# Blocks of x read by DMA already transposed, and another order of work in the last block, in a fused convolution and two-layer kernel

## The chip, the cores and the metric

The kernel runs on one core of one Trainium2 chip. The metric is device time in microseconds (us) of one execution, the median over several runs. Before the change it is 1195.06 us (three runs: 1194.38, 1195.06 and 1200.2). The profiled execution took 1194.39 us, of which the profile's span covers 1192.6 us.

## The reference

x has 2 x 4096 tokens of 192 features. Each of eight heads (24 features) has seven taps; softmax over the taps gives weights, and each token's feature is the weighted sum of itself and its six predecessors (zeros before the start of a sequence). Then come two feed-forward layers, 192 -> 2048 -> 192 each, with different functions between their products:

```python
x = attn_out.reshape(B * S, D)                  # causal 7-tap convolution of x
h = x @ w_in;  g = h * (1.0 / (1.0 + np.exp(-1.702 * h)));  x = g @ w_out
h = x @ w_in2; P = a[0] + a[1]*h + a[2]*h**2 + a[3]*h**3
Q = 1.0 + np.abs(b[0]) * np.abs(h) + np.abs(b[1]) * h**2
out = (P / (Q + 1e-06)) @ w_out2
```

## The kernel before, in words

The 8192 tokens are 16 blocks of 512 (T), numbered 0 to 15. Inside, features lie on partitions and tokens along the free dimension: a block is 128 features x 512 tokens ("main") and 64 features x 512 tokens ("side"), the latter folded to 128 x 256. So x must be transposed. `x_load` (L244) reads a block's rows as they are (one DMA of 256 KB, two of 64 KB) into `xn`; `x_halo` (L254) reads the six tokens ahead of the block, and of its second half, straight into the transposed tile `xt` by three DMAs with rearranged access patterns (L264 to L266); `x_transpose` (L269) turns the rest with six TensorE transposes (L275) and copies them from PSUM to `xt` with two ScalarE copies (L281, L282). `x_red` (L370) takes the block's largest magnitude from `xn` on VectorE (L373), `x_max` (L381) makes a scale of it, `x_conv_pool` (L325) does the convolution on GpSimd, and `x_high`, `x_low` (L403, L408) split the result into two halves of 16 bits.

Layer 1 is computed on split operands: `h_product` (L442) makes 128 x 1024 of a hidden product in one PSUM tile out of 24 matmuls (L423, L437); `gelu` and `g1_high`, `g1_low` follow; `o1_main` (L493) and `o1_side` (L504) make output product 1. Its result, rescaled by `scales` (L360) after a maximum over it (`x2_red_part` L556, `all_max` L83), is split by `high_part` and `low_part` (L347, L350) and enters layer 2: again `h_product`, then `unit` (L584: two ScalarE activations L591, L592, two VectorE operations L593, L594) and `denominator` (L597); `log` (L603) and `inverse` (L607), ScalarE functions of two different tables, and `quotient` (L611) give P / Q as a sigmoid of a logarithm; `o2_chunk` (L520) adds a sixteenth of output product 2 in float32 (L488). A hidden tile has eight steps (NS), a block sixteen chunks.

Work of several blocks is interleaved. All engines' orders are written by hand: each engine runs its instructions in the order in which the program issues them. The loop (L1003) has a turn for each block j from 0 to 14; with n1 = j+1, n2 = j+2 and conv = j+3, a turn holds:

- `x_load(conv)`, `x_halo(conv)` (L1007, L1008), all on the SP queue;
- the front part (`front_groups`, L763): hidden products of block n1 in layer 1 and of block j in layer 2, in groups of three PSUM tiles, with the chunks of block j-1 that are left. `extras` hangs further work on a step: `x_red(conv)` on step 2, `x_high(n2)` on 3, `x_low(n2)` on 4, `store(j-1)` on 6;
- the back part (`back_phase`, L803): `x_transpose(conv)` and `x_conv_pool(conv)`; output product 1 of n1 with the logarithms of block j beside it; scale and split of its result; the first products of the next front part; the quotients of block j.

On the SP queue the loads of a turn stand behind the `store` of the turn before, so they go out at the end of a front part, and what they bring is used in the next one. `xt` and `xn` have two buffers each. PSUM has eight banks: two for an output pair (`pair`, L302), six for three hidden tiles (`ps_h`).

The last turn calls `ending` (L654) instead of a back part. There output product 1 runs with all eight logarithms of block 14 beside it. Then the PSUM pool of three tiles is closed (L662) and replaced by two banks for block 14's output and two hidden tiles, so `product(i + 2)` waits for `readers(i)`:

```python
each(inverse, j, (0, 1))
quotient(j, 0)
o2_chunk(j, 0, 0)
```

After the split of x2, `product(i)` of block 15 alternates with one or two chunks of block 14 (L705 to L720); the quotients of block 15, its sixteen chunks and two half stores close the program.

Of the kernel before, what the change touches and what calls it, by code (L numbers as in the profile page):

```python
# [8 lines left out]
F32 = mybir.dt.float32  # L9
# [4 lines left out]
ALU = mybir.AluOpType  # L14
# [6 lines left out]
def kernel(  # L21
# [32 lines left out]
    tiny = ctx.enter_context(tc.tile_pool(name="tiny", bufs=3))  # L54
    ps_o = ctx.enter_context(tc.tile_pool(name="ps_o", bufs=1, space=bass.MemoryType.PSUM))

    ps_stack = ExitStack()
    ps_hs = [ps_stack.enter_context(tc.tile_pool(name="ps_h", bufs=3, space=bass.MemoryType.PSUM))]
    stack = ExitStack()
    stage = stack.enter_context(tc.tile_pool(name="stage", bufs=2))  # L60
    rings = []
# [192 lines left out]
    def x_halo(n, t=None):  # L254
# [11 lines left out]
        nc.sync.dma_start(out=t[D2:P, 0:HALO], in_=xf[first + TH - HALO:first + TH, P:D].rearrange("s d -> d s"))  # L266
        xt_t[n] = t

    def x_transpose(n):  # L269

        pt = ps_tile("pt")
        src, t = xn_t.pop(n), xt_t[n]

        def turn(dst, c):
            nc.tensor.transpose(out=dst, in_=src[:, c:c + P], identity=ident)  # L275

        for g in range(2):
            turn(pt[:, 1, g * P:(g + 1) * P], T + g * P)
        for g in range(NG):
            turn(pt[:, 0, g * P:(g + 1) * P], g * P)  # L280
        nc.scalar.activation(out=t[:, HALO:HALO + TH], in_=pt[:, 1, 0:TH], func=ACTF.Copy)  # L281
        nc.scalar.activation(out=t[:, 2 * HALO + TH:2 * HALO + W], in_=pt[:, 0], func=ACTF.Copy)  # L282
# [87 lines left out]
    def x_red(n):  # L370

        red = red_t[n] = tiny.tile([P, 2], F32, tag="red", name="red", bufs=4)
        nc.vector.tensor_reduce(  # L373
            out=red[:, 0:1], in_=xn_t[n], axis=AX.X, op=ALU.max, apply_absolute_value=True
        )
        if n * T % S:
            nc.vector.tensor_scalar(
                out=red[:, 1:2], in0=red[:, 0:1], scalar1=red_t[n - 1][:, 0:1], scalar2=None, op0=ALU.max
            )
# [140 lines left out]
    def o2_chunk(n, i, k, groups=range(NG)):  # L520
        pp = units_t[n][i][0]
        o_chunk(1, n, NS * k + i, ((pp, k, wo2[:, NS * k + i]),), groups)
# [27 lines left out]
    def x2_red(src):  # L550
        red = tiny.tile([P, 2], F32, tag="red2", name="red2")
        for j in range(2):
            x2_red_part(src, j, red)
        return red
# [48 lines left out]
    def log(n, i):  # L603
        qq = units_t[n][i][1]
        nc.scalar.activation(out=qq, in_=qq, func=ACTF.Ln, scale=ab[:, 15:16], bias=eps)  # L605
# [5 lines left out]
    def quotient(n, i):  # L611
        pp, qq = units_t[n][i]
        nc.vector.scalar_tensor_tensor(  # L613
            out=pp, in0=pp, scalar=ab[:, 0:1], in1=qq, op0=ALU.add, op1=ALU.mult
        )

    def each(f, n, steps):
        for i in steps:
            f(n, i)
# [33 lines left out]

    def ending(j, splits):  # L654

        n = j + 1
        for part in (o1_main, o1_side):
            for i in range(NS):
                o1_product(part, n, i, splits[i])
                if part is o1_main:  # L660
                    log(j, i)
        ps_stack.close()  # L662
        last = ctx.enter_context(tc.tile_pool(name="ps_last", bufs=1, space=bass.MemoryType.PSUM))
        po_t[1, j] = [last.tile([P, 512], F32, tag=f"l{k}", name="po") for k in range(2)]
        ps_hs.append(ctx.enter_context(tc.tile_pool(name="ps_two", bufs=2, space=bass.MemoryType.PSUM)))
        src = po_t.pop((0, n))
        each(inverse, j, (0, 1))
        quotient(j, 0)
        o2_chunk(j, 0, 0)
        pm = ps_tile("pm2")  # L670
        red = x2_red(src)
        all_max(red, pm)
        o2_chunk(j, 0, 1)
        sc = sc2_t[n] = tiny.tile([P, 24], F32, tag="sc2", name="sc2")
        scales(pm, sc, 2)
        xs = xs2_tiles(n)
        for p in (0, 1):
            high_part(src, sc[:, 1:2], xs, p)
        quotient(j, 1)
        for p in (0, 1):  # L680
            low_part(src, sc[:, 1:2], xs, p)
        each(inverse, j, (2, 3, 4, 5))
        x2_scales(sc, sc1_t.pop(n)[:, 6:7])
        each(quotient, j, (2, 3, 4, 5))
        phs = {}

        def product(i):
            phs[i] = h_product(1, n, i)

        def readers(i):  # L690
            pp = hl_tile().rearrange("p two t -> p (two t)").bitcast(F32)
            unit(n, phs.pop(i), pp)

        def own(m, i, groups=range(NG)):
            for k in range(2):
                o2_chunk(m, i, k, groups)

        first = NS // 2
        own(j, 1)
        rest = [lambda i=i, k=k: o2_chunk(j, i, k) for i in range(2, NS) for k in range(2)]  # L700
        product(0)
        rest.pop(0)()
        product(1)
        rest.pop(0)()
        for i in range(NS):  # L705
            readers(i)
            if i < 2:
                inverse(j, i + 6)
            if i + 2 < NS:
                product(i + 2)  # L710
            for f in rest[:2 if i > 2 else 1]:
                rest.pop(0)()
            denominator(n, i)
            if i < 2:
                quotient(j, i + 6)
            if i == first + 1:
                each(log, n, range(first))
            if i == NS - 2:
                each(inverse, n, (0, 1))
                quotient(n, 0)  # L720
        for f in rest:
            f()
        each(inverse, n, (2, 3))
        each(quotient, n, (1, 2, 3))
        store(j)
        each(log, n, range(first, NS))
        for i in range(first, NS):
            inverse(n, i)
            quotient(n, i)
        for i in range(NS - 1):  # L730
            own(n, i)
        for groups in (range(0, 2), range(2, 4)):
            own(n, NS - 1, groups)
        store_half(n, 0)
        store_half(n, 1)

    def front_phase(j, n1, extras):

# [64 lines left out]
    def back_phase(j, n1, n2, conv, splits):  # L803

        if conv is not None:
            x_transpose(conv)
            for k in range(K):
                x_conv_pool(conv, k)
        red = tiny.tile([P, 2], F32, tag="red2", name="red2")
        for part in (o1_main, o1_side):  # L810
            for i in range(NS):
                o1_product(part, n1, i, splits[i])
                if part is o1_main:
                    log(j, i)
            if part is o1_main:
                x2_red_part(po_t[0, n1], 0, red)
                if conv is not None:
                    x_max(conv)
                    x_scales(conv)
                    x_scale_out(conv)  # L820
        chunks = [lambda i=i, k=k: o2_chunk(j, i, k) for i in range(NS) for k in range(2)]
        each(inverse, j, (0, 1, 2, 3))
        src = po_t.pop((0, n1))
        pm = ps_tile("pm2")
        sc = sc2_t[n1] = tiny.tile([P, 24], F32, tag="sc2", name="sc2")
        x2_red_part(src, 1, red)

        def x2_ready():
            scales(pm, sc, 2)
            x2_split(n1, src, sc)  # L830

        early[n2, 0], early[n2, 1], second[n1, 0] = h_group(
            ((0, n2, 0), (0, n2, 1), (1, n1, 0)), lambda: all_max(red, pm), x2_ready
        )
        x2_scales(sc, sc1_t.pop(n1)[:, 6:7])
        each(quotient, j, (0, 1, 2, 3))
        each(inverse, j, (4, 5, 6, 7))
        for f in chunks[:3]:
            f()
        late_pe.extend(chunks[3:])  # L840
# [161 lines left out]
    with tc.manual_schedule():  # L1002
        for j in range(NB - 1):  # L1003
            n1, n2, conv = (j + d if j + d < NB else None for d in (1, 2, 3))
            extras = {i: [] for i in range(NS)}
            if conv is not None:
                x_load(conv)  # L1007
                x_halo(conv)  # L1008
                extras[2].append(lambda: x_red(conv))
            if j == 0:  # L1010
                xc_t[2] = pair("pc")
                for m in range(2 * K):
                    extras[m // 3].append(lambda m=m: x_conv_matmul(2, m))
                extras[5].append(lambda: x_high(2))
                extras[5].append(lambda: x_low(2))
            else:
                extras[NS - 2].append(lambda: store(j - 1))
                if n2 is not None:
                    extras[3].append(lambda: x_high(n2))
                    extras[4].append(lambda: x_low(n2))  # L1020
            splits = (front_groups if j else front_phase)(j, n1, extras)
            if n2 is None:
                ending(j, splits)
            else:
                back_phase(j, n1, n2, conv, splits)
# [27 lines left out]
```

## Time and profile before

| quantity | value |
|---|---|
| median of three runs | 1195.06 us |
| the profiled execution | 1194.39 us |
| its span | 1192.6 us |
| TensorE (PE) busy | 1174.6 us, 98% |
| VectorE (DVE) busy | 939.7 us, 79% |
| ScalarE (ACT) busy | 954.6 us, 80% |
| GpSimd (POOL) busy | 318.3 us, 27% |
| DMA moved | 27.86 MB in 55273 packets |

Times in the rows are microseconds from the start of the span unless ns is given. A timeline row gives start, duration, engine, line, operation, "out<-in" by tile names, shapes and a count of merged instructions; in brackets the idle time of the engine before it and what ended that. PE is TensorE's matmuls, PEld its weight loads, SPq a DMA issue on the SP queue. Merged matmuls overlap at their ends, so a matmul group's duration is slightly above its pace. A float32 matmul of L488 appears as two instructions: eight rows of count are one chunk.

### The profile page before, as it was taken

What the parts mean: (1) busy time and instruction counts of PE and PEld (TensorE: products, weight loads), DVE (VectorE), ACT (ScalarE), POOL (GpSimd) and SP (SyncE); (2) the same over time, 40 slices, a digit from 0 to 9 for tenths busy, and PEclk for the clock granted to TensorE, in tenths of its full rate; (3) what the DMA queues carried; (4) which work ended last, traced back from release to release, by engine and by line L of the source; (5) the groups of instructions that cost most, each with busy time, mean ns of one, the idle gap of its engine ahead of it and who ended that gap; (6) DMA issues with size and microseconds to landing.
All of it is one profiled execution on the core that took longest, in us unless ns stands there. A gap on an engine that the chain in (4) does not pass through costs nothing.

```text
span 1192.6 us, 24394 instructions
## 1 busy us (share of the span) xinstructions
PE 1174.6 (98%) x10693; PEld 952.3 (80%) x10693; DVE 939.7 (79%) x1034; ACT 954.6 (80%) x1025; POOL 318.3 (27%) x284
## 2 busy tenths in 40 slices
PE   8999999999999999999999999999999999999997
PEld 5547787978878788887878878797987879788676
DVE  6979796895968779596977959688795968859684
ACT  4656978879697887969788796978879798796875
POOL 0002805216070430607033070612407052000000
PEclk9999999999999999999999999999999999999999
DMA  8720001010010101001010100101001000000000
GB/s 239 230 58 1 1 2 28 1 28 1 2 28 1 28 1 28 2 2 28 1 28 2 28 1 1 29 1 28 1 9 21 1 14 1 14 2 1 15 1 27
DMA packets 55273, 27.86 MB, mean 23 GB/s; under 512 B 32896, under 2 KB 54400, under 8 KB 54400
## 3 DMA queue, kind: packets, MB, share of 16 engines
q1 hardware_dynamic: 54864, 26.31, 8.5%
q8 instruction: 83, 1.36, 0.5%
q14 instruction: 22, 0.18, 0.1%
q10 hardware_dynamic: 304, 0.00, 0.0%
HBM read 18.97 MB, written 6.29 MB: 21 GB/s over the span
## 4 chain that ended last, share of the span: by engine, by line
PE 91%; DVE 5%; ACT 3%; issue 1%; POOL 0%; ACTq 0%; POOLq 0%
PE ph L423 27%; PE po L488 26%; PE ph L437 14%; PE po L499 13%; PE po L509 7%; PE pc L321 2%; ACT qq L605 1%; PE pt L275 1%; DVE pp L613 1%; DVE hl L593 0%; PE pm L86 0%; DVE wm L216 0%; DVE qq L599 0%; ACT hl L592 0%; ACT qq L591 0%
## 5 line engine op out<-in xcount | busy, mean ns | idle before, releaser
L423 PE MATMUL ph<-xs,wm 128*128 128x256 f16 x3072 | 369.3, 273 | 0.7 <-ACT hl L527 0.4
L423 PEld LDWEIGHTS <-wm 128*128 128x128 f16 x3072 | 291.5, 98 | 60.5 <-issue 24.2
L488 PE MATMUL po<-wo,pp 128*128 128x192 f32 x1920 | 325.6, 326 | 1.7 <-DVE pp L613 1.7
L488 PEld LDWEIGHTS po<-wo,pp 128*128 128x128 f32 x1920 | 310.1, 190 | 3.1 <-DVE pp L613 1.3
L527 ACT ACTIVATE g<-ph,sc 128x1024 f32<-128x1024 f32 x120 | 132.5, 1116 | 108.0 <-PE ph L437 107.7
L591 ACT ACTIVATE qq<-ph,sc 128x1024 f32<-128x1024 f32 x128 | 142.7, 1115 | 67.3 <-PE ph L437 52.1
L593 DVE TENSOR_TENSOR pp<-pp,ph 128x1024 f32<-128x1024 f32 x120 | 145.7, 1214 | 60.4 <-ACT pp L592 60.3
L437 PE MATMUL ph<-xs,wr 64*128 64x256 f16 x3072 | 186.9, 270 | 3.6 <-DVE hl L594 2.6
L437 PEld LDWEIGHTS <-wr 64*128 64x128 f16 x3072 | 140.5, 94 | 43.4 <-issue 22.7
L613 DVE SCALAR_TENSOR_TENSOR pp<-pp,ab,qq 128x1024 f32<-128x1024 f32 x120 | 163.8, 1395 | 9.0 <-ACT qq L609 9.0
L599 DVE SCALAR_TENSOR_TENSOR qq<-qq,ab 128x1024 f32<-128x1024 f32 x128 | 166.4, 1301 | 0.0
L335 POOL TENSOR_TENSOR xc<-xc,tap 128x768 f32<-128x768 f32 x78 | 162.7, 2085 | 6.5
L331 POOL TENSOR_SCALAR xc<-xt,wt 128x512 f32<-128x512 f32 (+1 forms) x26 | 16.5, 647 | 551.9 <-ACT xt L282 551.9
L499 PE MATMUL po<-hl,wo 128*128 128x512 f16 x720 | 157.9, 379 | 0.0
L594 DVE SCALAR_TENSOR_TENSOR pp<-pp,sc,ph 128x1024 f32<-128x1024 f32 x120 | 153.6, 1280 | 4.3
L546 DVE SCALAR_TENSOR_TENSOR hl<-g,sc,hl 128x1024 f16<-128x1024 f32 x120 | 151.6, 1292 | 6.4 <-ACT hl L542 6.4
L605 ACT ACTIVATE qq<-qq,eps,ab 128x1024 f32<-128x1024 f32 x128 | 146.7, 1228 | 0.2
L592 ACT ACTIVATE pp<-ph,sc 128x1024 f32<-128x1024 f32 x120 | 145.0, 1208 | 0.0
L499 PEld LDWEIGHTS <-wo 128*128 128x128 f16 x720 | 70.1, 98 | 82.1 <-issue 0.4
L331 POOL TENSOR_SCALAR tap<-xt,wt 128x512 f32<-128x512 f32 (+1 forms) x156 | 128.2, 835 | 6.4
L609 ACT ACTIVATE qq<-qq 128x1024 f32<-128x1024 f32 x128 | 124.9, 1044 | 0.2
L542 ACT ACTIVATE hl<-g,sc 128x1024 f16<-128x1024 f32 x112 | 125.0, 1161 | 0.0
(101 smaller groups left out, 730.5 us busy)
## 6 DMA issues: line engine op xcount, KB each, us to landing
raw<-in_moe_w_out_dram SPq DMA_DIRECT2D x8, 768.0 KB, 7.5
out_dram<-on SPq DMA_DIRECT2D x15, 384.0 KB, 2.7
xn<-in_x_dram SPq DMA_DIRECT2D x16, 256.0 KB, 3.4
raw<-in_moe_w_in_dram SPq DMA_DIRECT2D x4, 1024.0 KB, 5.5
xn<-in_x_dram SPq DMA_DIRECT2D x32, 64.0 KB, 3.1
raw<-in_moe_w_in_dram SPq DMA_DIRECT2D x4, 512.0 KB, 8.0
wr<-wr SPq DMA_DIRECT2D x8, 128.0 KB, 2.3
xt<-in_x_dram SPq DMA_DIRECT2D x30, 1.5 KB, 2.6
```

The source lines that it names most:

```text
L335: nc.gpsimd.tensor_tensor(out=flat_of(c), in0=flat_of(c), in1=flat_of(d), op=ALU.add)
L423: nc.tensor.matmul(out=ph[:, h, k * TH:(k + 1) * TH], lhsT=wm[m][:, a_, f], rhs=xs[:, b_, h * TH:(h + 1) * TH], start=(start and k == 0 an ...
L437: nc.tensor.matmul(out=ph[:, h, k * TH:(k + 1) * TH], lhsT=wr[m][rows, a_, other, f], rhs=xs[rows, b_, :], start=(start and other == 0 and ...
L488: nc.tensor.matmul(out=dst, lhsT=tokens(t, k, g // 2)[:, g % 2 * P:(g % 2 + 1) * P], rhs=rhs, start=(done == 0 and g % 2 == 0 and q == 0), ...
L499: nc.tensor.matmul(out=po_t[0, n][0].rearrange("p (h t) -> p h t", h=2), lhsT=w[:, 0:P], rhs=all_tokens(t, k), start=(at == 1 and q == 0), ...
L546: nc.vector.scalar_tensor_tensor(out=hl[:, 1], in0=g, scalar=sc1_t[n][:, 4:5], in1=hl[:, 0], op0=ALU.mult, op1=ALU.subtract)
L592: nc.scalar.activation(out=pp, in_=h, func=ACTF.Identity, scale=sc[:, 7:8], bias=sc[:, 6:7])
L593: nc.vector.tensor_tensor(out=pp, in0=pp, in1=h, op=ALU.mult)
L594: nc.vector.scalar_tensor_tensor(out=pp, in0=pp, scalar=sc[:, 5:6], in1=h, op0=ALU.add, op1=ALU.mult)
L599: nc.vector.scalar_tensor_tensor(out=qq, in0=qq, scalar=ab[:, 14:15], in1=qq, op0=ALU.add, op1=ALU.mult)
L605: nc.scalar.activation(out=qq, in_=qq, func=ACTF.Ln, scale=ab[:, 15:16], bias=eps)
L613: nc.vector.scalar_tensor_tensor(out=pp, in0=pp, scalar=ab[:, 0:1], in1=qq, op0=ALU.add, op1=ALU.mult)
```

## The change

Three things. From block 4 on (turns with j of 1 and more) `x_load` and `x_transpose` fall away: the new `x_turned` reads the block from memory into `xt` with eight DMAs whose source access pattern swaps tokens and features, four of 128 x 128 and four of 64 x 128 elements of 4 bytes. `x_red` reads `xt` and stands on step 5 instead of step 2. And `ending` is written anew: output product 1 goes into one of the three hidden tiles, which stay open to the end; after half of its main part the order for ScalarE and VectorE is four logarithms, four inverses, four quotients of block 14, then the other four logarithms; the maximum over x2 is one reduction; one chunk stands behind each product.

```diff
@@ output pools @@
-    ps_stack = ExitStack()
-    ps_hs = [ps_stack.enter_context(tc.tile_pool(name="ps_h", bufs=3, space=bass.MemoryType.PSUM))]
+    ps_hs = [ctx.enter_context(tc.tile_pool(name="ps_h", bufs=3, space=bass.MemoryType.PSUM))]
@@ new, behind x_halo @@
+    def x_turned(n):
+        t, first = xt_t[n], n * T
+        for g in range(NG):
+            at = 2 * HALO + TH + g * P
+            nc.sync.dma_start(
+                out=t[:, at:at + P], in_=xf[first + g * P:first + (g + 1) * P, 0:P].rearrange("s d -> d s")
+            )
+            rows, at = slice(g // 2 * D2, (g // 2 + 1) * D2), HALO + g % 2 * P
+            nc.sync.dma_start(
+                out=t[rows, at:at + P], in_=xf[first + g * P:first + (g + 1) * P, P:D].rearrange("s d -> d s")
+            )
@@ x_red @@
-            out=red[:, 0:1], in_=xn_t[n], axis=AX.X, op=ALU.max, apply_absolute_value=True
+            out=red[:, 0:1], in_=xn_t[n] if n in xn_t else xt_t[n], axis=AX.X, op=ALU.max, apply_absolute_value=True
@@ ending @@
-        for part in (o1_main, o1_side):
-            for i in range(NS):
-                o1_product(part, n, i, splits[i])
-                if part is o1_main:
-                    log(j, i)
-        ps_stack.close()
...
-        each(inverse, j, (0, 1))
-        quotient(j, 0)
-        o2_chunk(j, 0, 0)
+        whole = ps_tile("po")
+        po_t[0, n] = [whole[:, 0], whole[:, 1]]
+        for part in (o1_main, o1_side):
+            for i in range(NS):
+                o1_product(part, n, i, splits[i])
+                if part is o1_main and i == half - 1:
+                    each(log, j, range(half))
+                    each(inverse, j, range(half))
+                    each(quotient, j, range(half))
+                    each(log, j, range(half, NS))
+        chunks = [lambda m=m, i=i, k=k: o2_chunk(m, i, k) for m in (j, n) for i in range(NS) for k in range(2)]
...
+        nc.vector.tensor_reduce(out=red, in_=flat_of(whole), axis=AX.X, op=ALU.max, apply_absolute_value=True)
         pm = ps_tile("pm2")
+        spare(1)
         all_max(red, pm)
+        spare(2)
...
         product(0)
-        rest.pop(0)()
+        each(inverse, j, (half, half + 1))
+        each(quotient, j, (half, half + 1))
+        spare(1)
         product(1)
-        rest.pop(0)()
         for i in range(NS):
             readers(i)
-            if i < 2:
-                inverse(j, i + 6)
+            if i == 0:
+                each(inverse, j, (half + 2, half + 3))
+            spare(1)
             if i + 2 < NS:
                 product(i + 2)
-            for f in rest[:2 if i > 2 else 1]:
-                rest.pop(0)()
             denominator(n, i)
-            if i < 2:
-                quotient(j, i + 6)
-            if i == first + 1:
-                each(log, n, range(first))
-            if i == NS - 2:
-                each(inverse, n, (0, 1))
-                quotient(n, 0)
+            if i == 0:
+                each(quotient, j, (half + 2, half + 3))
+            if i == 4:
+                each(log, n, range(half))
+            if i == 5:
+                each(inverse, n, (0, 1))
+                each(quotient, n, (0, 1))
+            if i == 6:
+                each(inverse, n, (2, 3))
+                quotient(n, 2)
+        spare(16 - (32 - len(chunks)))
...
@@ back_phase @@
-            x_transpose(conv)
+            if conv in xn_t:
+                x_transpose(conv)
@@ the loop over turns @@
-                x_load(conv)
-                x_halo(conv)
-                extras[2].append(lambda: x_red(conv))
+                if j:
+                    x_halo(conv)
+                    x_turned(conv)
+                else:
+                    x_load(conv)
+                    x_halo(conv)
+                extras[5 if j else 2].append(lambda: x_red(conv))
```

`spare(c)` issues the next c of the 32 chunks of blocks 14 and 15. After the loop come the rest of block 14's chunks, the last quotient of the first half of block 15, its other logarithms, inverses and quotients, `store(14)`, and block 15's chunks and half stores.

## Rows read from the trace of the kernel before

**Rows 1.** The page: the chain that ended last, by engine.

```profile
PE 91%; DVE 5%; ACT 3%; issue 1%; POOL 0%; ACTq 0%; POOLq 0%
```

**Rows 2.** Busy time by engine (with counts), PE clock, DMA share, GB/s, one turn.

```profile
400.21:470.58 70.37, 70.37 (x669) 58.49 (x665) 55.25 (x59) 58.96 (x62) 23.79 (x22) 1.00 0.05 12
```

**Rows 3.** Timeline of the same turn: transposes, output product 1, VectorE behind it.

```profile
400.41 0.87 PE L275 MATMUL pt<-ident,xn 128*128 128x128 f32 x6
...
401.12 10.52 PE L499 MATMUL po<-hl,wo 128*128 128x512 f16 x48
...
411.68 0.69 DVE L558 TENSOR_REDUCE red<-po 128x1 f32<-128x512 f32 x1 [4.75 <-PE po L499]
```

**Rows 4.** Timeline of PE: output product 1 of block 14, in the turn without transposes.

```profile
1033.83 6.43 PE L499 MATMUL po<-hl,wo 128*128 128x512 f16 x29
```

**Rows 5.** SP queue, halo issues of one turn.

```profile
332.10 0.41 SPq L264 DMA_DIRECT2D xt<-in_x_dram  x1
...
333.21 0.62 SPq L266 DMA_DIRECT2D xt<-in_x_dram  x1
```

**Rows 6.** Timeline, end of a front part: around steps 4 to 6 and the store.

```profile
464.49 1.01 DVE L343 SCALAR_TENSOR_TENSOR xs<-xc,sc,xs 128x768 f16<-128x768 f32 x1
...
466.75 1.22 DVE L593 TENSOR_TENSOR pp<-pp,ph 128x1024 f32<-128x1024 f32 x1
...
470.58 0.38 SPq L636 DMA_DIRECT2D out_dram<-on  x1
```

**Rows 7.** DMA queue of 329.8:336.5 (packets, MB, share of 16 engines): store, load, halo.

```profile
q1 hardware_dynamic: 3184, 0.79, 55.1%
```

**Rows 8.** DMA queue of 334.2:335.6: halo packets alone.

```profile
q1 hardware_dynamic: 1025, 0.00, 39.9%
```

**Rows 9.** DMA queue of 9.8:10.1: halo packets queued up behind loads.

```profile
q1 hardware_dynamic: 737, 0.01, 140.6%
```

**Rows 10.** DMA queue of 333.9:334.4: halo packets as they are issued, at their densest.

```profile
q1 hardware_dynamic: 671, 0.01, 75.8%
```

**Rows 11.** Busy time by engine, three stretches of the ending behind output product 1.

```profile
1119.30:1126.87 7.57, 5.86 (x36) 5.35 (x36) 6.30 (x12) 3.90 (x6) 0.00 (x0) 1.00 0.00 1
1126.87:1161.80 34.93, 32.16 (x283) 27.25 (x283) 29.25 (x25) 27.27 (x29) 0.00 (x0) 1.00 0.00 1
1161.80:1192.60 30.80, 22.55 (x136) 21.66 (x134) 15.71 (x14) 17.70 (x19) 0.00 (x0) 1.00 0.08 26
```

**Rows 12.** Timeline of the ending, in order of time.

```profile
1103.40 10.53 PE L499 MATMUL po<-hl,wo 128*128 128x512 f16 x48
...
1107.04 9.17 ACT L605 ACTIVATE qq<-qq,eps,ab 128x1024 f32<-128x1024 f32 x8
...
1116.22 1.28 ACT L609 ACT_TABLE_LOAD   x1
...
1120.04 1.54 PE L488 MATMUL po<-wo,pp 128*128 128x192 f32 x8 [0.74 <-DVE pp L613]
...
1126.87 0.83 PE L437 MATMUL ph<-xs,wr 64*128 64x256 f16 x12
...
1128.95 1.47 PE L488 MATMUL po<-wo,pp 128*128 128x192 f32 x8
...
1131.39 1.22 DVE L593 TENSOR_TENSOR hl<-hl,ph 128x1024 f32<-128x1024 f32 x1 [1.30 <-ACT hl L592]
...
1135.04 1.28 DVE L613 SCALAR_TENSOR_TENSOR pp<-pp,ab,qq 128x1024 f32<-128x1024 f32 x1
...
1164.85 2.87 PE L488 MATMUL po<-wo,hl 128*128 128x192 f32 x16 [1.84 <-DVE hl L613]
...
1170.27 18.47 PE L488 MATMUL po<-wo,hl 128*128 128x192 f32 x112 [2.55 <-DVE hl L613]
...
1175.17 3.90 ACT L609 ACTIVATE qq<-qq 128x1024 f32<-128x1024 f32 x4
```

**Rows 13.** The page: DMA queue of the instructions (packets, MB, share of 16 engines).

```profile
q8 instruction: 83, 1.36, 0.5%
```

More of the change, by code (lines that the diff above doesn't have):

```diff
@@ L654, in ending @@
     def ending(j, splits):
-        n = j + 1
+        n, half = j + 1, NS // 2
+        whole = ps_tile("po")
+        po_t[0, n] = [whole[:, 0], whole[:, 1]]
         for part in (o1_main, o1_side):
@@ L659, in ending, with spare @@
                 o1_product(part, n, i, splits[i])
-                if part is o1_main:
-                    log(j, i)
-        ps_stack.close()
[L663 to L666, printed above, removed]
-        each(inverse, j, (0, 1))
-        quotient(j, 0)
-        o2_chunk(j, 0, 0)
+                if part is o1_main and i == half - 1:
[3 more added lines that the diff above has]
+                    each(log, j, range(half, NS))
+        del po_t[0, n]
+        chunks = [lambda m=m, i=i, k=k: o2_chunk(m, i, k) for m in (j, n) for i in range(NS) for k in range(2)]
+        def spare(count):
+            for _ in range(count):
+                chunks.pop(0)()
+        red = tiny.tile([P, 1], F32, tag="red2", name="red2")
+        nc.vector.tensor_reduce(out=red, in_=flat_of(whole), axis=AX.X, op=ALU.max, apply_absolute_value=True)
         pm = ps_tile("pm2")
-        red = x2_red(src)
+        spare(1)
         all_max(red, pm)
-        o2_chunk(j, 0, 1)
+        spare(2)
         sc = sc2_t[n] = tiny.tile([P, 24], F32, tag="sc2", name="sc2")
-        scales(pm, sc, 2)
+        scales(pm, sc)
         xs = xs2_tiles(n)
[L677 to L682, printed above, removed]
+        for p in (1, 0):
+            high_part(whole, sc[:, 1:2], xs, p)
+        for p in (1, 0):
+            low_part(whole, sc[:, 1:2], xs, p)
         x2_scales(sc, sc1_t.pop(n)[:, 6:7])
-        each(quotient, j, (2, 3, 4, 5))
         phs = {}
@@ L692, in readers @@
             unit(n, phs.pop(i), pp)
[L694 to L700, printed above, removed]
         product(0)
-        rest.pop(0)()
+        each(inverse, j, (half, half + 1))
+        each(quotient, j, (half, half + 1))
+        spare(1)
         product(1)
-        rest.pop(0)()
         for i in range(NS):
             readers(i)
-            if i < 2:
-                inverse(j, i + 6)
+            if i == 0:
+                each(inverse, j, (half + 2, half + 3))
+            spare(1)
             if i + 2 < NS:
                 product(i + 2)
-            for f in rest[:2 if i > 2 else 1]:
-                rest.pop(0)()
             denominator(n, i)
-            if i < 2:
-                quotient(j, i + 6)
-            if i == first + 1:
-                each(log, n, range(first))
-            if i == NS - 2:
-                each(inverse, n, (0, 1))
-                quotient(n, 0)
[L721 to L727, printed above, removed]
+            if i == 0:
[3 more added lines that the diff above has]
+            if i == 5:
+                each(inverse, n, (0, 1))
+                each(quotient, n, (0, 1))
[3 more added lines that the diff above has]
+        spare(16 - (32 - len(chunks)))
+        whole = ps_tile("po")
+        po_t[1, n] = [whole[:, 0], whole[:, 1]]
+        quotient(n, 3)
+        each(log, n, range(half, NS))
+        for i in range(half, NS):
             inverse(n, i)
             quotient(n, i)
-        for i in range(NS - 1):
-            own(n, i)
+        store(j)
+        spare(len(chunks) - 2)
         for groups in (range(0, 2), range(2, 4)):
-            own(n, NS - 1, groups)
-        store_half(n, 0)
-        store_half(n, 1)
+            for k in range(2):
+                o2_chunk(n, NS - 1, k, groups)
+        for k in range(2):
+            store_half(n, k)
     def front_phase(j, n1, extras):
```

## The prediction

> **What bounds the kernel.** I read the chain of waits first: TensorE is 91% of the chain that ended last [rows 1]. Then the engines' busy time over one turn, from store to store: TensorE is busy in all of its 70.37 us, at the full clock (1.00, which is 2.4 GHz), ScalarE in 58.96, VectorE in 55.25, GpSimd in 23.79, and the DMA engines in 5% [rows 2]. So a turn is as long as TensorE's list of instructions; time taken off that list comes back in full, and work moved among the other engines costs nothing while their slack lasts. The ending is different: there TensorE has gaps that wait for VectorE [rows 11, 12]. The DMA queue, idle now, is what the change loads, so its rows decide the sign.
>
> **Transposes removed.** In a turn, six transposes start at 400.41 and output product 1 at 401.12: 0.71 us of TensorE's list [rows 3]. A check from the other side: output product 1 of block 14 starts at 1033.83 [rows 4], that of block 15 at 1103.40 [rows 12], 69.57 us later with no transposes between; that is 0.80 less than 70.37 [rows 2], with the one matmul of a maximum missing there too, about a sixth of 0.71. Blocks 4 to 15 are 12 blocks: 12 x 0.71 = **8.5 us**, with ends 12 x (0.80 - 0.12) = 8.2 and 12 x 0.80 = 9.6. The two ScalarE copies that go are hidden behind TensorE and give nothing. A later `x_red` costs VectorE what it did, and VectorE waits 4.75 us for TensorE in each back part [rows 3], which covers it.
>
> **DMA added.** One burst of the old turn holds one store (512 rows of 768 bytes), the load (512 + 2 x 256 runs) and three halo reads (1536 elements): 3072, and with 16 more per DMA for seven DMAs 3184, the count in the row [rows 7]. So an element of the transposed read is one packet. A block then is 512 x 192 = 98304 packets instead of 1024. Three prices:
> - Alone, 1025 halo packets fill 39.9% of 16 engines for 1.4 us: 0.399 x 16 x 1400 / 1025 = 8.7 ns each [rows 8]. At one after another on each engine a block takes 98304 x 8.7 / 16 = 53.6 us.
> - Queued up behind loads, 737 go in 0.3 us, with packets of an engine overlapping (140.6%) [rows 9]: 2457 per us, a block in 40 us.
> - As they are issued, at the densest, 671 go in 0.5 us, with the engines 75.8% filled [rows 10]: 1342 per us, 73 us.
>
> The first takes the engines as full and without overlap; large DMAs should fill them, since the third price shows engines that wait for issues of at most 768 packets. I take 54 us and keep 40 and 73.
>
> Until when must it land? The SP queue issues the halo reads behind the store, from 332.10 to 333.83, 1.7 us [rows 5]; eight more issues of about 0.6 overlap with the transfer. With some 2 us from an issue to its packets (an estimate: the halo's are densest from 333.9, 1.8 us behind the issue at 332.10 [rows 5, 10]), the block is there some 3.7 us + 54 behind the store. The next store follows 70.37 us after the last one [rows 2]. `x_red` on step 5 comes behind step 4's `x_low`, at 464.49, and one more denominator, so before the next group's first operation at 466.75, 66 us behind the store that let the reads out [rows 2, 6]. So 54 + 3.7 = 58 is in time. Up to 62 us of transfer nothing waits; between 62 and 67 VectorE is late at `x_red`, but by no more than its 4.75 us of idle time [rows 3]; behind it on VectorE stand the next unit's operations, which free hidden tiles, and output product 1 waits for those. Past 67 us TensorE waits. The next store's DMA issue, at 470.58, stands behind [rows 6]; the store's data queues with the reads, but its tile isn't needed again for a turn. GpSimd's convolution starts when its old input is free, at about 465.5 [rows 6], with the data already there. Cost taken: **0**.
>
> [...]
>
> **The ending.** I laid out TensorE's, ScalarE's and VectorE's lists in the new order by hand, with prices of the rows: a logarithm 9.17 / 8 = 1.15 us, an inverse 3.90 / 4 = 0.97, a table load 1.28, three VectorE operations 1135.04 - 1131.39 = 3.65, a chunk 18.47 / 14 = 1.3, a product 1128.95 - 1126.87 = 2.08 [rows 12]. The same done for the old order ends TensorE at 1188.4; the trace ends at 1170.27 + 18.47 = 1188.74 [rows 12]. In the old clock:
> - Output product 1 runs from 1103.40 to 1119.30 [rows 11, 12]. Now eight logarithms end at 1116.21, a table load follows, and the first chunk waits for its quotient until 1120.04 [rows 12]. In the new order four logarithms end at 1107.04 + 4.6 = 1111.6, table and four inverses at 1116.8, the quotients at 1118.9: four steps' chunks are ready when output product 1 ends. The other logarithms hold ScalarE until 1122.7, so the split, and `product(0)`, come at 1123.8 instead of 1126.87 [rows 12], with three chunks done instead of four: 3.1 - 1.3 = 1.8 gained. TensorE's idle time there is 7.57 - 5.86 = 1.7 [rows 11].
> - In the loop VectorE needs 3.65 per step and TensorE 2.08 + 1.3 = 3.4. A third tile lets TensorE start ahead, then VectorE sets the pace: waits of 1.9 and three of 0.3 us in my list, against 3.8 in the old order's: 1.0 gained.
> - At the end the old order runs out of block 14's chunks and waits 1.84 and 2.55 us for the first quotients of block 15 [rows 12] (5.0 in my list, which counts weight loads). One chunk per product leaves four chunks for this time; block 15's first four quotients come between 1156 and 1167.5, its chunks from 1160, and one wait of 1.0 us for the fifth remains: 4.0 gained.
>
> TensorE's last chunk ends at 1181.6, so **6.8 us** is gained. Ends: nothing at all, if ScalarE's order costs elsewhere what it gives; and all idle time there, 1.7 + (34.93 - 32.16) + (30.80 - 22.55 less 3.9 behind the last chunk) = 8.9 [rows 11].
>
> **The sum.** 1194.39 - 8.5 - 6.8 = 1179.1 against the profiled execution. That execution lies 0.67 below the median of 1195.06, so I say 1179.8. The forecast's own range is 1194.4 - 9.6 - 8.9 = 1176 to 1194.4 - 8.2 - 0 = 1186, in the profiled execution's time.
>
> **Rivals.**
> 1. *The transposed read doesn't fit into a turn* (slower). Place: `x_red` on VectorE, with TensorE starved of hidden tiles behind it. It decides from 67 us per block, 98304 / 67 = 1467 packets per us. At 1342 per us [rows 10] a block's 73 us, 1.1 for 1536 halo packets and 1.4 for the store, half of that burst's rest [rows 7], make a turn of 75.5: 5.1 more than 70.37, in some 12 turns 61; with the ending 1194.4 + 61 - 6.8 = 1249. If each turn's reads also wait for the store behind the late `x_red`, 470.58 - 466.75 = 3.8 more per turn [rows 6], 1295. For it: no row shows more than about 1000 such packets in a row, and reads with a stride can slow down when they go on. Against it: the packets' own time, and rows 9. Chance 0.22.
> 2. *The ending gains nothing*, since VectorE's pace in the loop decides, and the third tile only moves the waits. Against it: the waits of 1.84 and 2.55 are gone by the order alone. 1194.4 - 8.5 + 0.7 = 1186.6. Chance 0.08.
> 3. *The reads hold up the instructions' own fetches*: 83 packets of some 16 KB [rows 13], which share the DMA engines with the reads in 12 of 15 turns, so some 66. At half a microsecond of TensorE's wait for each, 33 us, which more than takes back the gain: 1179.8 + 33 = 1213; at a fifth, 1193. Nothing in the rows shows such a wait. Chance 0.08.
>
> **How the numbers follow.** The forecast has 0.62. What a measurement of this kernel can tell from no change is 0.5%, 6 us: 1189 to 1201. Faster: the forecast, rival 2 and a little of rival 3, 0.71. Same: a part of rival 3 and a mild rival 1, 0.06. Slower: 0.23. The range of 8 in 10 takes the forecast, rival 2, nearly all of rival 3 and the mildest of rival 1: from 1174 to 1213. Cases of both signs hold weight: the likeliest one's own range, around 1180, is 1176 to 1187.
>
> **What would show it.** In the changed profile a turn from store to store should be 69.7 us with TensorE busy throughout; L275 should be gone from block 4 on; the DMA row should show some 1.2 million packets, and the DMA share in the middle slices should be some eight tenths; the last DMA of a block should land some 58 us behind the store, and `x_red` should have no idle time in front. TensorE's last chunk should end some 7 us nearer to the start of output product 1 than before. I am wrong if VectorE shows idle time before `x_red` that a DMA ended, if DMA engines are full through whole turns, or if the waits of the ending come back at another line.

## The result, and the profile after

The changed kernel takes 1180.0 us (median of five runs, 1179.17 to 1180.75), the kernel before 1195.14 on the same occasions: a ratio of 0.9866, interval [0.9847, 0.9884]. That is 15.1 us, 1.3%, faster; the forecast was 1179.8. The profiled execution took 1180.75 us, with a span of 1179.0.

The page of the changed kernel: busy time of the first engines, the DMA share in 40 slices, the queue that carries the reads.

```profile
PE 1166.8 (99%) x10620; PEld 944.5 (80%) x10620; DVE 935.2 (79%) x1033; ACT 948.0 (80%) x1003; POOL 321.0 (27%) x284
...
DMA  8724996999999999999999999999999920000000
...
q1 hardware_dynamic: 1223184, 26.32, 89.7%
```

Some 1.2 million packets instead of 55 thousand, and DMA engines that are busy through nearly the whole kernel; yet TensorE's share went up to 99%. One turn, from store to store (span of the window, then PE, PEld, DVE, ACT and POOL busy, PE clock, DMA share, GB/s), answers to [rows 2]:

```profile
329.72:399.41 69.69, 69.69 (x663) 57.83 (x659) 55.38 (x60) 58.20 (x60) 23.66 (x21) 1.00 1.21 13
```

69.69 us instead of 70.37, TensorE busy in all of it: 0.68 us per turn, where 0.71 was forecast. The DMA share above 1 means that packets of one engine overlap. The end of the front part, timeline, answers to [rows 3, 6]:

```profile
394.64 0.96 DVE L385 TENSOR_REDUCE red<-xt 128x1 f32<-128x780 f32 x1
...
398.85 0.83 PE L449 MATMUL ph<-xs,wr 64*128 64x256 f16 x12
...
399.41 0.39 SPq L648 DMA_DIRECT2D out_dram<-on  x1
...
399.62 10.53 PE L511 MATMUL po<-hl,wo 128*128 128x512 f16 x48
...
410.19 0.69 DVE L570 TENSOR_REDUCE red<-po 128x1 f32<-128x512 f32 x1 [3.56 <-PE po L511]
```

Output product 1 follows the last hidden product at once, without transposes between. The reduction over x (now L385) has no idle time in brackets: the block was there. The SP queue of the same turn shows how it came:

```profile
329.72 0.39 SPq L648 DMA_DIRECT2D out_dram<-on  x1
...
332.08 0.61 SPq L273 DMA_DIRECT2D xt<-in_x_dram  x1
332.74 8.62 SPq L277 DMA_DIRECT2D xt<-in_x_dram  x1
341.40 4.76 SPq L273 DMA_DIRECT2D xt<-in_x_dram  x1
...
376.61 10.55 SPq L277 DMA_DIRECT2D xt<-in_x_dram  x1
399.41 0.39 SPq L648 DMA_DIRECT2D out_dram<-on  x1
```

The first issue takes 0.61 us, the later ones 4.4 to 10.8: the SP queue is held up in them until 387.2. When the transfer ends is read from the DMA line of 385:399, whose 40 slices are 0.35 us each, and from the row of the block's last DMA there (KB, us from its issue to the signal that it has landed):

```profile
DMA  9993221019989999999000000000100000000000
...
xt<-in_x_dram SPq DMA_DIRECT2D x1, 32.0 KB, 16.7
```

Busy up to the 19th slice, 391.7. From the issue at 332.08 that is 59.6 us for 98304 packets: 1650 per us, 9.7 ns per packet on each of 16 engines. That is a mean over an uneven stream. The DMA queue of two single microseconds in it, 360.08:361.08 and 371.08:372.08 (packets, MB, share of 16 engines):

```profile
q1 hardware_dynamic: 2596, 0.01, 157.7%
...
q1 hardware_dynamic: 211, 0.00, 23.5%
```

The last packets end 62 us behind the store at 329.72. The signal, 16.7 us behind the issue at 376.61, comes at 393.3, which is 64 behind the store; the reduction comes 65 behind it, so 1.3 us are to spare. Other turns have less. VectorE in the turn from 747.81:

```profile
813.09 0.96 DVE L385 TENSOR_REDUCE red<-xt 128x1 f32<-128x780 f32 x1 [0.28 <-DMA xt<-in_x_dram]
```

Here the reduction waits for the DMA, and in two more of the 12 turns it has 0.2 us of idle time in front. So at `x_red` the reads are just in time, with no margin; what keeps TensorE from waiting is VectorE's idle time behind it (measured below, with one more read).

The ending, timeline, answers to [rows 12]:

```profile
1095.21 0.88 ACT L644 ACTIVATE on<-po 128x384 f32<-128x384 f32 x2
...
1099.96 4.64 ACT L617 ACTIVATE qq<-qq,eps,ab 128x1024 f32<-128x1024 f32 x4
1104.61 1.28 ACT L621 ACT_TABLE_LOAD   x1
...
1112.15 1.57 PE L500 MATMUL po<-wo,pp 128*128 128x192 f32 x8
...
1117.26 0.40 PE L449 MATMUL ph<-xs,wr 64*128 64x256 f16 x4 [0.29 <-DVE xs L363]
...
1131.94 0.83 PE L449 MATMUL ph<-xs,wr 64*128 64x256 f16 x12 [1.12 <-DVE hl L606]
...
1152.75 10.56 PE L500 MATMUL po<-wo,hl 128*128 128x192 f32 x64
...
1164.13 10.67 PE L500 MATMUL po<-wo,hl 128*128 128x192 f32 x64 [0.82 <-DVE hl L625]
```

In the kernel before, ScalarE's copy for the same store, and who ended TensorE's waits in 1100:1193 (us in total, times, longest), by groups that lie behind the loop over the steps of `ending`, in it and ahead of it:

```profile
1102.29 0.88 ACT L632 ACTIVATE on<-po 128x384 f32<-128x384 f32 x2
...
PE po L488 <- DVE hl L613: 4.4, 2, 2.5
PE ph L437 <- DVE hl L594: 2.6, 2, 1.3
PE po L488 <- DVE pp L613: 1.7, 2, 1.0
```

The first chunk (L500 at 1112.15) starts without a wait. TensorE's last chunk ends at 1174.8. From the ScalarE copy of the last store ahead of the ending (1095.21 here) to the end of the span are 83.8 us; in the kernel before that copy starts at 1102.29 and the stretch is 90.3. So the ending gained 6.5 us. The first store is issued at 190.36 here and at 189.06 before; over ten profiles, of kernels with the reads and without, it lies between 189.06 and 190.42 (189.06 in e7, with them, 189.75 in e2, without), so these 1.3 us are scatter. From the first to the last store before the ending are thirteen turns, before and after (columns as above):

```profile
189.06:1103.19 914.13, 914.13 (x8642) 759.74 (x8638) 720.09 (x754) 764.96 (x803) 281.21 (x242) 1.00 0.05 12
190.36:1096.12 905.76, 905.76 (x8571) 751.60 (x8566) 715.41 (x754) 755.88 (x779) 278.24 (x237) 1.00 1.02 12
```

TensorE is busy throughout both, and they took 914.13 us before and 905.76 after: 8.4 less. Together: 8.4 + 6.5 - 1.3 = 13.6, the difference of the two spans.

### The profile page after: what moved, and what is told of

Read it like the earlier page. It is cut to its first block, busy times and chain, and to the rows that moved or that the text cites. A ratio compares the mean times of both kernels' runs of the same rounds, so it can differ in the third digit from the quotient of the medians.

```text
span 1179.0 us, 24317 instructions
## 1 busy us (share of the span) xinstructions
PE 1166.8 (99%) x10620; PEld 944.5 (80%) x10620; DVE 935.2 (79%) x1033; ACT 948.0 (80%) x1003; POOL 321.0 (27%) x284
## 4 chain that ended last, share of the span: by engine, by line
PE 90%; DVE 5%; ACT 4%; issue 1%; POOL 0%; ACTq 0%; POOLq 0%
PE ph L435 27%; PE po L500 26%; PE ph L449 14%; PE po L511 13%; PE po L521 7%; PE pc L333 2%; ACT qq L617 1%; ACT qq L621 1%; DVE hl L605 0%; PE pm L85 0%; DVE wm L215 0%; DVE hl L625 0%; DVE qq L611 0%; DVE hl L606 0%; ACT qq L603 0%
## 5 line engine op out<-in xcount | busy, mean ns | idle before, releaser
L435 PE MATMUL ph<-xs,wm 128*128 128x256 f16 x3072 | 369.3, 273 | 0.7 <-ACT hl L539 0.4
L435 PEld LDWEIGHTS <-wm 128*128 128x128 f16 x3072 | 291.6, 98 | 60.5 <-issue 24.3
L500 PE MATMUL po<-wo,pp 128*128 128x192 f32 x1920 | 325.3, 326 | 0.0
L500 PEld LDWEIGHTS po<-wo,pp 128*128 128x128 f32 x1920 | 310.1, 190 | 1.1 <-issue 0.2
L343 POOL TENSOR_SCALAR xc<-xt,wt 128x512 f32<-128x512 f32 (+1 forms) x26 | 27.4, 1064 | 532.6 <-DVE xs L355 484.8
L558 DVE SCALAR_TENSOR_TENSOR hl<-g,sc,hl 128x1024 f16<-128x1024 f32 x120 | 157.6, 1342 | 4.2 <-ACT hl L554 3.8
L625 DVE SCALAR_TENSOR_TENSOR pp<-pp,ab,qq 128x1024 f32<-128x1024 f32 x120 | 151.9, 1298 | 6.7 <-ACT qq L621 6.7
L347 POOL TENSOR_TENSOR xc<-xc,tap 128x768 f32<-128x768 f32 x78 | 153.0, 1962 | 6.5
L554 ACT ACTIVATE hl<-g,sc 128x1024 f16<-128x1024 f32 x112 | 124.9, 1160 | 0.0
```

What stands on the lines that cost most here:

```text
L343: nc.gpsimd.tensor_scalar(out=part_of(d, j), in0=src, scalar1=wt[:, j, k:k + 1], scalar2=1.0, op0=ALU.mult, op1=ALU.mult)
L347: nc.gpsimd.tensor_tensor(out=flat_of(c), in0=flat_of(c), in1=flat_of(d), op=ALU.add)
L435: nc.tensor.matmul(out=ph[:, h, k * TH:(k + 1) * TH], lhsT=wm[m][:, a_, f], rhs=xs[:, b_, h * TH:(h + 1) * TH], start=(start and k == 0 an ...
L500: nc.tensor.matmul(out=dst, lhsT=tokens(t, k, g // 2)[:, g % 2 * P:(g % 2 + 1) * P], rhs=rhs, start=(done == 0 and g % 2 == 0 and q == 0), ...
L558: nc.vector.scalar_tensor_tensor(out=hl[:, 1], in0=g, scalar=sc1_t[n][:, 4:5], in1=hl[:, 0], op0=ALU.mult, op1=ALU.subtract)
L625: nc.vector.scalar_tensor_tensor(out=pp, in0=pp, scalar=ab[:, 0:1], in1=qq, op0=ALU.add, op1=ALU.mult)
```

## The experiments

**The two parts alone.** One kernel has the reads with the old ending, one the new ending with the old loads and transposes.

```diff
 e1: the function ending, and the pool ps_h, as before
 e2: x_load, x_halo, x_transpose, x_red on step 2 in all turns, as before
```

> The transposed reads from block 4 on and the later x_red, with the ending of before. My theory (TensorE's list sets a turn, the reads land in time): a turn of 69.7 us instead of 70.37, 12 turns, so 8.3 us faster than the kernel before: 1186.8. Rival (the reads cost something in other stretches, for instance by holding up instruction fetches or loads, and the ending gained more than 6.5): 1189 to 1192. Rival (the reads gave all of it): 1180.

> The new ending alone; x of all blocks is loaded and transposed on TensorE as before. My theory (the ending's 6.5 us come from its own order and need nothing of the reads): from the start of output product 1 of block 15 to the end 82.7 us instead of 89.2, so 1195.1 - 6.5 = 1188.6, turns of 70.4 unchanged. Rival (the ending gains only because the reads leave ScalarE and GpSimd less to do): 1194 to 1195.

Measured: 1187.52 us (ratio 0.9935, [0.9922, 0.9947]) and 1188.91 (0.9945, [0.9931, 0.9959]); the kernel before beside them 1195.22. The reads give 7.7, the ending 6.3, together 14.0 of 15.1: within the intervals, some 1.5 us either way, the parts add up and don't need each other. Stretch of the ending in e2: 84.0 us, as after the change. The reads alone are 0.7 short of the expectation, and their profile shows where. The last 112 matmuls of L488 [rows 12] took 18.47 us before; with the same ending in e1 they took 20.15, and the window of the end says why:

```profile
1162.36:1186.20 23.84, 20.14 (x112) 19.84 (x112) 7.76 (x7) 9.25 (x10) 0.00 (x0) 0.93 0.05 17
```

The mean granted clock is 0.93 instead of 1.00: behind the old ending's waits of 1.84 and 2.54 us TensorE's clock fell for a part of this stretch. The same waits stand in the kernel before, whose profile shows 1.00 [rows 11], so these waits don't always bring it.

**The deadline.** x_red back to step 2:

```diff
-                extras[5 if j else 2].append(lambda: x_red(conv))
+                extras[2].append(lambda: x_red(conv))
```

> As after the change, but x_red stands on step 2, where it was before, so that VectorE comes to it some 49 us behind the store that lets the reads out. My theory (a block takes 60 to 62 us to transfer, so VectorE waits 12 to 13 us there, of which 5 to 7 are covered by its slack and by the tiles that are already free): 6 to 9 us more in each of 12 turns, 1252 to 1288, and the profile shows VectorE waiting at the reduction for the DMA. Rival (what counts is only that the reads fit into a turn, and VectorE's slack covers the rest): 1180 to 1185.

Measured, in one run: 1373.0 us, 193 more than after the change, 16 per turn. The direction is that of my theory, the size is not. One turn runs from 452.84 to 538.94 (86.1 us); timeline of the wait:

```profile
517.02 0.97 DVE L385 TENSOR_REDUCE red<-xt 128x1 f32<-128x780 f32 x1 [15.88 <-issue]
...
520.49 1.47 PE L449 MATMUL ph<-xs,wr 64*128 64x256 f16 x12 [14.44 <-DVE pp L606]
...
521.89 2.65 PE L435 MATMUL ph<-xs,wm 128*128 128x256 f16 x12
```

VectorE waits 15.88 us for the block, which arrives 64 us behind the store (here the profile names no releaser, in nine of the 12 turns it names the DMA), and 14.44 of that reach TensorE: right behind step 2's reduction stand the operations that free a hidden tile, and TensorE runs only one group ahead. The slack that I had counted on was not there. The rest is the clock. Windows of the wait and of what follows:

```profile
506.00:520.40 14.40, 0.05 (x2) 0.00 (x0) 3.34 (x4) 2.65 (x3) 0.00 (x0) 0.66 0.82 5
520.40:525.00 4.60, 4.51 (x28) 3.26 (x28) 4.60 (x5) 0.43 (x1) 0.00 (x0) 0.57 0.00 0
```

Behind 14 us of idling TensorE works on at 0.57, near the lower of its two levels (1.2 instead of 2.4 GHz): twelve matmuls of L435 that take 1.48 us at full clock took 2.65. A step-2 reduction was harmless only as long as x came in a few microseconds.

**One more read, three more reads.** Reads into tiles that nobody reads, ahead of each block's own:

```diff
+        for g in range(1):     # three in e4_extra3
+            nc.sync.dma_start(out=junk_t[g], in_=xf[first + g * P:first + (g + 1) * P, 0:P].rearrange("s d -> d s"))
```

> As after the change, with one more transposed read of 128 x 128 elements into a tile that nobody reads, issued ahead of each block's eight: 116224 packets per block instead of 99840. My theory (some 1640 packets per us, so a block lands 71 + 2 us behind the store, 8 us late at x_red, of which 4.75 are VectorE's slack): 3 to 5 us more in each of 12 turns, 1216 to 1240. Rival (only the queue's throughput counts, 71 us and the store against a turn of 69.7): 2 to 2.5 us per turn, 1204 to 1210. Rival (there is room for more reads): 1180.

> As after the change, with three more transposed reads of 128 x 128 elements of 4 bytes per block into tiles that nobody reads: 148992 packets per block. Theory (a turn becomes as long as a block's transfer and its latency, some 1640 packets per us): 91 + 2 us and up to 4 for the store behind, so turns of 93 to 97 us, with a TensorE that loses clock in its waits; 1460 to 1530. Rival (reads beyond a turn are partly absorbed): under 1400.

Measured with one: 1217.09 us (ratio 1.018, [1.0162, 1.0199]), 37 more than after the change, 3.1 in each of 12 turns: the first theory. The reduction now waits, in the timeline of one turn:

```profile
410.32 0.97 DVE L388 TENSOR_REDUCE red<-xt 128x1 f32<-128x780 f32 x1 [8.23 <-issue]
...
417.03 2.32 PE L514 MATMUL po<-hl,wo 128*128 128x512 f16 x10 [1.93 <-DVE hl L561]
```

Of 8.23 us on VectorE 1.93 reach TensorE there, at output product 1, whose last operands are late; other waits come behind it. Over the run VectorE waits 87.5 us at this reduction, 7.3 for each of 12 turns, of which 3.1 are lost. So on step 5 there is a slack of some four microseconds, close to the 4.75 of the prediction.

With three, in one run: 1427.6 us, 32 below the expected range. Two stores of the SP queue:

```profile
467.66 4.68 SPq L651 DMA_DIRECT2D out_dram<-on  x1
558.57 4.62 SPq L651 DMA_DIRECT2D out_dram<-on  x1
```

A turn is 90.9 us, and 148992 packets / 90.9 = 1639 per us. The DMA share over this turn is 1.39. The few microseconds for latency and for the store that I had added don't appear, since the SP queue issues the next block's first reads (472.45) before the reduction of this one starts (474.83). Here, far past the limit, a turn is as long as its packets; just past it, with one more read, a turn of 72.8 us (69.7 + 3.1) is 1.9 longer than 116224 packets at this rate.

**Packets or bytes.** The same number of extra packets, with 8 bytes each:

```diff
+        for g in range(4):
+            nc.sync.dma_start(
+                out=junk_t[g][0:96].rearrange("p (s two) -> p s two", two=2),
+                in_=xf[first + g * P:first + (g + 1) * P].rearrange("s (p two) -> p s two", two=2),
+            )
```

> As e4_extra3, but the 49152 extra packets per block carry 8 bytes each (two neighbouring features, 96 partitions) instead of 4. Theory (the price is per packet, not per byte): the same time as e4_extra3 within 20 us. Rival (per byte): twice the extra transfer, turns of some 120 us, over 1750.

Measured, in one run each: 1426.35 us, against 1427.6. Twice the extra bytes cost nothing; between 4 and 8 bytes the price is per packet.

**The parts of the ending.** The prediction gave 1.8 us to the early quotients of block 14, 1.0 to the third tile, 4.0 to one chunk per product. Before these runs I wrote the lists out again with one part undone at a time, which gave other values; both are in the expectations.

```diff
 e6: all eight logarithms of block 14 within output product 1, its inverses and quotients behind it
-            spare(1)                      # e7, in the loop
+            spare(2 if 2 < i < 7 else 1)
 e8: logarithms of block 15 on step 5, two inverses and one quotient on step 6, the rest behind the loop
 e10: pools of before (two hidden tiles), order of after
 e12: as e6, the third chunk behind the split
 e13: order of before, pool of three hidden tiles kept open
```

> As after the change, but within output product 1 all eight logarithms of block 14 come first, as before; its first two inverses and first quotient stand behind output product 1, the second quotient and the next two inverses and quotients around the split. The stretch from the last full store before the ending to the end of the span is 82.9 us after the change and 89.4 before it. First theory (the prediction's terms): the early quotients are worth 1.8 us, so 84.7, 1181.8 in all. Rival (the three lists written out again by hand, with this part alone undone): the first chunk waits 0.7 us, and later waits shrink by nearly nothing, so 83.6, 1180.7.

> As after the change, but from step 3 to step 6 of the ending's loop two chunks of block 14 stand behind a product instead of one, so that they run out earlier, as before. First theory (the prediction's terms: the spread of the chunks is worth up to 4.0 us): the stretch of 82.9 us becomes 86 to 87, 1183 to 1184 in all. Rival (lists by hand with this part undone): the waits inside the loop shrink by what the wait for block 15's quotients grows, 82.9, 1180.

> As after the change, but block 15's first four logarithms, inverses and quotients stand where they stood before: logarithms on step 5, two inverses and one quotient on step 6, the others behind the loop. First theory (the prediction's terms: the end gains by the spread of the chunks): 0 to 1 us, 82.9 to 83.9. Rival (lists by hand): TensorE waits 2.7 us for the second quotient of block 15, in all 2.2 more: 85.1, 1182.2 in all.

> The ending in its new order, but with the PSUM tiles of before: output product 1 in the output pair, the pool of three hidden tiles closed, two hidden tiles and two banks for block 14's output opened, the maximum over x2 in two reductions. First theory (the prediction's terms: the third tile is worth 1.0 us): the stretch of 82.9 us becomes 84, 1181 in all. Rival (lists by hand): products wait for the readers of two products earlier, 2.5 and 2.7 us at steps 2 and 3 and 4.5 at step 7, where block 15's quotients now stand ahead of a tile's readers on VectorE; in all 6.9 more: 89.8, 1187 in all, as slow as the ending of before.

> As e6_logs_first, with the third chunk moved behind the split, so that the second quotient stands ahead of every chunk that reads it. Theory (lists by hand): the first chunk waits 0.7 us for its quotient and the third comes later; from the last full store's copy before the ending to the end of the span 84 to 85.5 us against 83.8 after the change. Rival (the prediction's term): 85.6.

> The ending in its old order, but with the three hidden tiles kept open: output product 1 and block 15's output each in one of them, block 14's output in the output pair; the transposed reads as after the change. Theory (lists by hand): the waits inside the loop go (0.5, 1.5, 1.5, 0.3 us), the waits for quotients stay, 3.7 us better than the old ending: from the last full store's copy to the end of the span 86.6 us against 90.3 (before) and 83.8 (after), 1183 in all. Rival (the prediction's term): 1.0 better, 89.3, 1185.5 in all.

In e6 one chunk reads the second step's numerator ahead of its quotient: it leaves out a wait that its result needs, and e12 has that wait, so e12 is the one to read. In the expectations of e6, e7, e8 and e10 the stretch starts with the store's issue, 0.9 us behind ScalarE's copy: 82.9 there is 83.8 here. Measured, with the stretch from the last store's copy to the end of the span of the profiled execution:

| kernel | us | ratio to before, interval | stretch | TensorE's waits there |
|---|---|---|---|---|
| before | 1195.14 | | 90.3 | 0.74, 0.97; 1.29, 1.29; 1.84, 2.55 |
| after | 1180.0 | 0.9866 [0.9847, 0.9884] | 83.8 | 0.29; 1.12; 0.82 |
| e6 | 1180.57 | 0.9873 [0.9854, 0.9892] | 84.8 | 0.65, 1.30; 0.37; 0.82 |
| e12 | 1180.12 | 0.9877 [0.9861, 0.9894] | 84.2 | 0.65, 0.84; none; 0.82 |
| e7 | 1179.53 | 0.9866 [0.985, 0.9883] | 83.8 | 0.29; 1.11; 0.90 |
| e8 | 1183.08 | 0.9895 [0.9877, 0.9913] | 86.0 | 0.29; 1.12; 0.31, 2.48 |
| e10 | 1188.39 | 0.9938 [0.9922, 0.9955] | 91.5 | none; 2.41, 0.87, 4.33; none |
| e13 | 1185.63 | 0.9921 [0.9906, 0.9936] | 89.2 | 0.64, 0.97; none; 1.94, 2.48 |

(Waits ahead of the loop; in it; behind it.) The lines behind three of them, of e8, e10 and e13 in turn, timelines of PE:

```profile
1152.18 2.84 PE L500 MATMUL po<-wo,hl 128*128 128x192 f32 x16 [0.31 <-DVE hl L625]
1157.50 18.47 PE L500 MATMUL po<-wo,hl 128*128 128x192 f32 x112 [2.48 <-DVE hl L625]
```

```profile
1125.22 1.06 PE L450 MATMUL ph<-xs,wr 64*128 64x256 f16 x12 [2.41 <-DVE hl L607]
1131.26 0.83 PE L450 MATMUL ph<-xs,wr 64*128 64x256 f16 x12 [0.87 <-DVE hl L607]
1150.06 1.46 PE L450 MATMUL ph<-xs,wr 64*128 64x256 f16 x12 [4.33 <-DVE hl L607]
```

```profile
1154.75 2.84 PE L500 MATMUL po<-wo,hl 128*128 128x192 f32 x16 [1.94 <-DVE hl L625]
1160.07 20.15 PE L500 MATMUL po<-wo,hl 128*128 128x192 f32 x112 [2.48 <-DVE hl L625]
```

What follows. One chunk per product is worth nothing with the other edits in place (e7); without the earlier quotients it was not tried. The early quotients of block 14 are worth 0.4 (e12) by the stretch, too little for the median times to tell. The earlier quotients of block 15 are worth 2.2 (e8): the old wait of 2.5 us is back, that of 1.84 is not (0.31). The third tile is worth 7.7 in the new order (e10; 5.4 of it are waits, and behind them the clock was 0.92 over 1125 to 1150 and 0.85 over 1150 to 1160), more than the whole ending gained, since block 15's quotients then stand on VectorE ahead of the operations that free a tile. In the old order it is worth less. e13's 89.2 missed the 86.6 of my lists and is the number of the rival, 89.3, but not for the rival's reason: e13 lost clock at its end, as e1 did. Against e1's stretch of 91.8, which has the same reads, the same old order, two tiles and the same loss of clock, it is 2.6 less; those are the two waits of 1.29. So the order and the tile depend on each other: the tile is what makes the earlier quotients affordable. Undone one at a time, the edits don't add up to the 6.5 us, and which of them removed the wait of 1.84 is not shown.

## Why the prediction was right, and where it was not

- *The number.* 1179.8 against 1180.0 is nearer than the working deserves: the two profiled executions differ by 13.6 us where the terms sum to 15.3, and runs of the changed kernel alone lie up to 1.6 us apart. That part is luck.
- *A turn is TensorE's list.* Right: 69.69 us, TensorE busy in all of it; 8.4 us over the turns against 8.5. That leaves nothing for ScalarE's copies, as said.
- *The reads fit.* Right for TensorE, but with no margin at `x_red`, where the prediction had 8 us. The term was mis-sized: 54 us for a block, 58 behind the store; measured 60 to 62, and 64 behind the store, of which about 1.5 pass between the last packets and the signal, which the prediction left out. I had taken the packets' own time in a short burst, 8.7 ns, as if it were the pitch. In a long stream packets overlap (the share of 1.21 in the turn), and the pitch is 9.7 ns. The Trainium skill has under "DMA: Bandwidth & Descriptors", section "Bandwidth", some 10.5 ns per packet for a transfer of 4 KB issued from GpSimd, and does not say on how many engines; taken as the time on one engine, which the Trainium skill doesn't say, it would lie 8% above what this trace shows, while the burst's row lay 10% below. The burst behind loads [rows 9] said little about a stream: it shows a rate that lasted 0.3 us, and this stream has such microseconds too, 2596 packets in one and 211 in another.
- *The signs of being wrong.* Two that the prediction named came: idle time before `x_red` that a DMA ended (0.28 us in one turn), and DMA engines full through whole turns (1.21 where eight tenths were expected). The gain came all the same. The signs were set too tight: idle time of VectorE costs nothing until it reaches TensorE, and it did not.
- *The limit at 67 us.* Its place was right, x_red on VectorE. One more read, 71 us, cost 3.1 us per turn, so a slack of about four was there on step 5. As a property of VectorE's idle time it was too general: on step 2 nearly nothing of a wait is covered (e3). What covers a late reduction is what stands right behind it in its engine's order.
- *Rival 1.* It did not come; e5 and e4 show it just beyond: 16% more packets are enough. Its price far past the limit is simpler than I wrote: a turn as long as its packets, at 1640 per us, without the store's 3.8 us (e4).
- *Rival 3.* The instructions' own packets were no trouble: no wait of TensorE in the thirteen turns.
- *The ending.* Sum right (6.5 against 6.8), and right by stretches of TensorE's waits: ahead of the loop 1.71 became 0.29, in it 2.6 became 1.1, behind it 4.4 became 0.8, so 1.4, 1.5 and 3.6 against 1.8, 1.0 and 4.0. The step that failed is the sentence that put the last 4.0 down to "one chunk per product": e7 shows that edit to be worth nothing beside the others, e8 that block 15's quotients moved forward bring 2.2 of it, and e10 that they need the third tile; what brings the rest is open. The sum could hold because the lists behind it had these moves in them: block 15's first quotients stand in the prediction with their times. Rival 2's picture, waits that only move, is what the new order gives without the third tile (e10, 91.5 us against 90.3).

## What to carry to other kernels

Work of TensorE that a DMA can do in the background is worth its full price where TensorE sets the time, as long as the stream ends ahead of its reader; count packets, not bytes, take their price from a long stream and add the time from the last packet to its signal, and look at what stands behind the reader on its engine. A sum over a chain of waits can be right while the reason given for a term is wrong: undo one edit at a time before carrying it over. A buffer and an order may be worth little apart and much together.

## What the runs showed of the hardware

- A transposed read of 4-byte elements runs at some 1640 to 1650 packets per us over 16 engines in a long stream (59.6 us for the 98304 packets of a block, 90.9 for 148992), and extra packets of 8 bytes cost the same as extra ones of 4 (1426.35 and 1427.6 us). Single microseconds of the stream hold from 211 to 2596 packets.
- From a block's last packets to the signal that lets its reader start about 1.5 us passed (391.7 to 393.3).
- The SP queue is held up by such reads: 0.6 us for the first issue, then 4 to 11 us for each, until the stream has nearly drained; a store behind them waits (1.7 us in its issue in one of e5's turns, 4.7 in e4's).
- The DMA share goes above 1 in such a stream (1.21 over a turn), since packets of an engine overlap.
- TensorE's clock fell behind waits as short as those in the ending in some kernels' profiles (0.93 over the last 24 us in e1, behind 1.84 and 2.54 us) and not in others (1.00 before, behind 1.84 and 2.55), and to 0.57 behind 14 us of idling in e3.
